# Attention scan with two gated MLPs on one core: key and query transposes on 128 rows, a new instruction order, and repeated weight checks moved to other tiles

## The chip, the cores and the metric

The kernel runs on one core of one Trainium2 chip. The metric is device time in microseconds; shown are three runs of the kernel before and one profiled execution. Engines are named as in the profile: PE (TensorE), PEld (its weight loads), DVE (VectorE), ACT (ScalarE), POOL (GpSimd), SP (SyncE, which issues most DMAs).

## The reference

Shapes: batch 4, 8 heads, 768 steps, head size 48; then 3072 tokens of width 384 through two MLPs of inner width 1536 and 2048. Inputs and weights are float32 (weights handed to the kernel as 64-bit words).

```python
mag = np.sqrt(a_re*a_re + a_im*a_im)
scale = np.minimum(mag, 0.999) / (mag + 1e-06)
a_re_n, a_im_n = a_re*scale, a_im*scale
for t in range(S):                       # S_re, S_im: [B, H, D, D]
    new_re = ar*S_re - ai*S_im           # ar, ai: row t of a_re_n, a_im_n
    new_im = ar*S_im + ai*S_re
    S_re, S_im = new_re + einsum('bhd,bhe->bhde', k[t], v[t]), new_im
    y[:, :, t] = einsum('bhd,bhde->bhe', q[t], S_re)
x = y as [tokens, 384]
xn = x / sqrt(mean(x*x) + 1e-06) * rms_g
x = (silu(xn @ w_gate) * (xn @ w_val)) @ w_out
h = x @ w_in
out = (h * clip(h + 3, 0, 6) / 6) @ w_out2
```

## The kernel before, in words

**Units.** The 768 steps are cut into seven units, each of two chunks of C steps (C is 32 in the first and last unit, 64 in the others). Inside a chunk the products of the complex factors a are accumulated forwards and backwards from its middle, so each chunk has two halves of C/2 steps. All 128 partitions work on a unit at once: a partition is one combination of half, batch, head and chunk. Before the change the partition number counts, from its highest bit down, g (batches 0-1 or 2-3), half, head parity, chunk, batch within g, and head within parity.

**Preparation of a unit (DVE and ACT).** `steps_norm` scales a; `steps_scan` runs C/2 dependent multiply-add steps (lines 442 and 446), inverts the products (`sq`, `k1`, `k2`) and forms the scaled keys and queries in two arrays P and X2 (`x1`, `x2`), of 48 real and 48 imaginary values at columns 0 to 47 and 64 to 111, hence 112 columns per step. `kwrite` writes the key part to DRAM (k_dr), and `load_k` loads it back with steps on partitions.

**Attention of a unit (`steps_G`).** `tr` turns P and X2 by TensorE: it fills one PSUM tile psT (512 columns) with eight transposes of 64 partitions (one g) by 112 columns, and ACT copies the tile to XTt (lines 597 and 603). A unit of 64-step chunks has 16 such tiles, the two short ones 8 each, 96 in all. `scores` (psS), `sums` (psU: keys times values), `state` (DVE, with a swap of the halves of the state by DMA), `outs` (psY), a normalising `scale`, and `flip` (psX: three 128-row transposes, and a split of the result into a high and a low part xh, xl) follow. psT, psS, psX and psF (the transposed chunk factors) take turns in a ring of two PSUM tiles; psU and psY share one.

**First gated projection (`steps_M`).** For each 256 tokens it multiplies by the 12 gate and value tiles, each product as three matmuls of high and low parts (`mm3`, lines 735 to 737, tile pm: 792 calls of three within the ordered part); `silu` writes the result u to DRAM.

**Order.** All of this is cut into 1680 steps, many of them generators with several parts. A string ORDER, two characters per call, gives the sequence of 2654 calls in which the parts are emitted, and the order of each engine's queue is the order of emission.

**After the units.** `steps_out1` (the first MLP's output projection) loads u in tiles uu, splits it into uh and ul (line 905), and multiplies; `steps_moe2` does the second MLP over six blocks of 512 tokens. For each of 16 inner tiles j of a block, `up` gives ph (9 matmuls), `act` computes r on ACT (line 948), r on DVE (949), gh on ACT (950) and gl on DVE (951), and `down` (9 matmuls) follows two tiles later. Tiles r, gh and gl are in rings of two. This part is ordered by the framework's scheduler.

**Checks.** The weights arrive as 64-bit words, and a check of their range (line 311: the smallest magnitude of a tile of words, to a column of wmin) guards the fast path. The gate and value weights are checked by loading them again: `recheck` loads 384 words per partition (rawc) into the ring of three buffers T1 to T3 and reduces them; 24 of these are listed beside the second MLP's blocks 1 and 2. `verdict` collects all flags and writes one column to DRAM after block 3, `verdict_end` reads it back as a row after block 4. If a flag were set, a slow fallback would run after all this.

## Time and profile before

| what | us |
|---|---|
| median of three runs | 1140.67 (1138.0 to 1144.91) |
| profiled execution | 1143.95 |
| span of its trace | 1141.9 |
| PE busy | 1061.2 (93%) |
| DVE busy | 777.4 (68%) |
| ACT busy | 543.5 (48%) |
| POOL busy | 73.9 (6%) |

The rest of the page, cut to two of its parts. The first shows busy tenths in 40 equal slices of the span, with the granted TensorE clock in tenths of full speed; the second is the chain of work that ended last, by engine.

```profile
PE   0457999999999999999999999999999999999997
...
DVE  7999999999998987868888885533333333333332
ACT  4655777758667574623334442332332333333332
...
PEclk9999999999999999999999999999999999999999
...
PE 67%; DVE 13%; issue 8%; DMA 7%; ACT 3%; POOL 1%; SPq 1%; DVEq 0%; ACTq 0%; POOLq 0%
```

A slice is 28.5 us. The first three are the preparation of the first unit, up to about the twentieth the attention of the other units runs beside the first gated projection, and then follow the output projection and the second MLP.

### The profile page before, as it was taken

Reading aid. Unit: us, or ns where it says so; the run is one execution under the profiler, and the core shown is the slowest. Engines: PE = TensorE matmul, PEld = TensorE weight load, DVE = VectorE, ACT = ScalarE, POOL = GpSimd, SP = SyncE. Lnnn points to the kernel's source line nnn. Section 1 sums busy time; section 2 is a strip of 40 time slices with the busy share of each in tenths; the row PEclk is TensorE's granted clock in tenths of the full one; section 3 lists DMA queues with packets and bytes.
Section 4 is the critical chain, followed back from the end, with each engine's and each line's share of the span. In section 5 each row is a group of like instructions: output and inputs, shape, how many; then the busy total and the mean of one; then the engine's idle time right before and its main releaser. Section 6 shows DMA issues by size and latency. Waiting matters only on the chain.

```text
span 1141.9 us, 24599 instructions
## 1 busy us (share of the span) xinstructions
PE 1061.2 (93%) x10264; PEld 926.9 (81%) x10264; DVE 777.4 (68%) x1501; ACT 543.5 (48%) x930; POOL 73.9 (6%) x99
## 2 busy tenths in 40 slices
PE   0457999999999999999999999999999999999997
PEld 0457899999998999999988886788888888888885
DVE  7999999999998987868888885533333333333332
ACT  4655777758667574623334442332332333333332
POOL 3010010000000010001222220000000000000000
PEclk9999999999999999999999999999999999999999
DMA  7525628437456365455765448601200310200000
GB/s 307 156 56 187 178 75 242 120 109 241 119 178 170 91 193 139 118 156 137 222 211 178 131 144 263 130 1 39 73 28 1 96 43 1 83 10 1 28 1 31
DMA packets 81434, 133.72 MB, mean 117 GB/s; under 512 B 32225, under 2 KB 50786, under 8 KB 80674
## 3 DMA queue, kind: packets, MB, share of 16 engines
q1 hardware_dynamic: 80658, 131.95, 39.0%
q8 instruction: 82, 1.34, 0.5%
q14 instruction: 38, 0.31, 0.1%
q10 hardware_dynamic: 656, 0.11, 0.1%
HBM read 89.77 MB, written 34.60 MB: 109 GB/s over the span
## 4 chain that ended last, share of the span: by engine, by line
PE 67%; DVE 13%; issue 8%; DMA 7%; ACT 3%; POOL 1%; SPq 1%; DVEq 0%; ACTq 0%; POOLq 0%
PE po L736 9%; PE po L737 9%; PE po L735 9%; PE pm L735 6%; PE pm L736 5%; PE pm L737 5%; PE ph L735 5%; PE ph L737 5%; PE ph L736 5%; DMA rawc<-in_wgv_dram 3%; PE psT L597 2%; PE psY L687 2%; DMA u_dr<-sg 1%; PE psS L650 1%; PE psU L667 1%
## 5 line engine op out<-in xcount | busy, mean ns | idle before, releaser
L735 PE MATMUL pm<-xh,wg 128*128 128x256 f32 x864 | 254.4, 294 | 0.5 <-ACT xh L717 0.4
L736 PE MATMUL pm<-xl,wg 128*128 128x256 f32 x864 | 245.6, 284 | 1.8 <-DVE xl L719 1.8
L737 PE MATMUL pm<-xh,wg 128*128 128x256 f32 x864 | 245.0, 284 | 0.0
L735 PEld LDWEIGHTS pm<-xh,wg 128*128 128x128 f32 x864 | 165.2, 191 | 5.8 <-issue 0.9
L736 PEld LDWEIGHTS pm<-xl,wg 128*128 128x128 f32 x864 | 165.6, 192 | 2.2 <-DVE xl L719 2.2
L737 PEld LDWEIGHTS pm<-xh,wg 128*128 128x128 f32 x864 | 165.5, 192 | 0.2
L949 DVE SCALAR_TENSOR_TENSOR r<-r,ph 128x512 f32<-128x512 f32 x96 | 65.8, 685 | 99.3 <-ACT r L948 99.1
L951 DVE TENSOR_TENSOR gl<-r,gh 128x512 fp32r<-128x512 f32 x96 | 67.5, 703 | 92.4 <-ACT gh L950 92.3
L950 ACT ACTIVATE gh<-r 128x512 fp32r<-128x512 f32 x96 | 60.7, 632 | 122.8 <-PE po L737 83.5
L948 ACT ACTIVATE r<-ph,biasz 128x512 f32<-128x512 f32 x96 | 65.8, 687 | 105.4 <-PE ph L737 105.1
L736 PE MATMUL po<-gl,w_h 128*128 128x512 f32 x288 | 113.9, 396 | 1.1 <-DVE gl L951 1.1
L737 PE MATMUL po<-gh,w_l 128*128 128x512 f32 x288 | 113.9, 395 | 0.0
L735 PE MATMUL ph<-x2b,wi_h 128*128 128x512 f32 x288 | 113.5, 395 | 0.4 <-DVE r L949 0.4
L737 PE MATMUL ph<-x2b,wi_l 128*128 128x512 f32 x288 | 113.4, 394 | 0.0
L736 PE MATMUL ph<-x2b,wi_h 128*128 128x512 f32 x288 | 113.2, 393 | 0.0
L735 PE MATMUL po<-gh,w_h 128*128 128x512 f32 x288 | 108.1, 395 | 0.0
L905 DVE TENSOR_TENSOR ul<-uu,uh 128x512 fp32r<-128x512 f32 x72 | 51.5, 717 | 73.2 <-ACT uh L904 73.1
L736 PE MATMUL po<-ul,wo 128*128 128x512 f32 x216 | 85.1, 394 | 3.0 <-DVE ul L905 3.0
L904 ACT ACTIVATE uh<-uu 128x512 fp32r<-128x512 f32 x72 | 45.4, 631 | 88.2 <-PE po L737 75.6
L737 PE MATMUL po<-uh,wo 128*128 128x512 f32 x216 | 84.7, 393 | 0.0
L442 DVE TENSOR_TENSOR m<-LAt,P 128x192 f32<-128x192 f32 x192 | 68.2, 355 | 3.9 <-ACT LAt L412 0.2
L603 ACT ACTIVATE XTt<-psT 112x512 f32<-112x512 f32 x96 | 55.2, 593 | 28.3 <-PE psT L597 27.8
(130 smaller groups left out, 1956.8 us busy)
## 6 DMA issues: line engine op xcount, KB each, us to landing
u_dr<-sg SPq DMA_DIRECT2D x72, 256.0 KB, 3.7
uu<-u_dr SPq DMA_DIRECT2D x72, 256.0 KB, 2.7
raw<-in_wo_dram SPq DMA_DIRECT2D x28, 384.0 KB, 3.6
wraw<-in_wgv_dram SPq DMA_DIRECT2D x12, 768.0 KB, 7.6
S<-in_s_all_dram SPq DMA_DIRECT2D x24, 384.0 KB, 3.8
rawc<-in_wgv_dram SPq DMA_DIRECT2D x24, 384.0 KB, 3.9
K<-k_dr SPq DMA_DIRECT2D x40, 224.0 KB, 4.2
LAt<-in_a_all_dram SPq DMA_DIRECT2D x5, 1536.0 KB, 9.4
```

What stands on the lines that cost most here:

```text
L442: tt(out=m4, in0=la, in1=pj, op=ALU.mult)
L597: nc.tensor.transpose(ps[:XW, i * 64:(i + 1) * 64], src, ident[g * 64:(g + 1) * 64, g * 64:(g + 1) * 64])
L603: nc.scalar.activation(d, s, AF.Copy)
L735: nc.tensor.matmul(ps, lhsT=wh, rhs=xh, start=first, stop=False)
L736: nc.tensor.matmul(ps, lhsT=wh, rhs=xl, start=False, stop=False)
L737: nc.tensor.matmul(ps, lhsT=wl, rhs=xh, start=False, stop=last)
L904: nc.scalar.activation(uh, uu, AF.Copy)
L905: (nc.gpsimd if n < 0 else nc.vector).tensor_tensor(out=ul, in0=uu, in1=uh.bitcast(F32), op=ALU.subtract)
L948: nc.scalar.activation(r, ph, AF.Relu, bias=biasz[:, 2:3], scale=sixth)
L949: stt(out=r, in0=r, scalar=1.0, in1=ph, op0=ALU.min, op1=ALU.mult)
L950: nc.scalar.activation(gh, r, AF.Copy)
L951: tt(out=gl, in0=r, in1=gh.bitcast(F32), op=ALU.subtract)
```

## The change

- The partition number counts half first, then g. Keys and queries of both g's for one half then lie in 64 neighbouring partitions, and `tr` transposes all 128 partitions at once: four transposes of 128 x 112 fill a psT tile. XTt has two parts (keys, queries) of 64 column groups instead of three of 32, and `col`, `kwrite` and `emit_F` index accordingly. In `steps_G` all transposes of a unit are listed before its first scores.
- ORDER is another string for another sequence of as many calls (2654).
- `recheck` loads 256 words per partition, 36 times, into the ring of tile r in the second MLP, one after each of the tiles j of blocks 1, 2 and, in part, 3. `verdict` and `verdict_end` both follow block 4.

```diff
--- before.py
+++ after.py
@@ -31,40 +31,40 @@
 
 DIGITS = "0123456789abcdefghijklmnopqrstuvwxyzABCDEFGHIJKLMNOPQRSTUVWXYZ+-"
-ORDER = (
...
+ORDER = (
...
 )
 ON_POOL = set()
 
@@ -247,7 +247,7 @@
     gcol = const.tile([128, KT], F32, name="gcol")
     flags = const.tile([128, 11 * NU], F32, name="flags")
     nc.vector.memset(flags, 0.0)
-    NW = 3 * J1 + 2 * J2
+    NW = 4 * J1 + 2 * J2
     wmin = const.tile([128, NW], F32, name="wmin")
     nc.vector.memset(wmin, 1.0)
     biasz = const.tile([128, 5], F32, name="biasz")
@@ -494,7 +494,7 @@
         def kwrite(half, sp):
             sl = slice(sp * hs, (sp + 1) * hs)
             for g in range(2):
-                p0 = g * 64 + half * 32
+                p0 = half * 64 + g * 32
                 src = P[p0:p0 + 32, 1 + sp * hs:1 + (sp + 1) * hs] if half == 0 else X2[p0:p0 + 32, sl]
                 nc.sync.dma_start(k_dr[u, g, :, half * HC + sp * hs:half * HC + (sp + 1) * hs], src)
         X = lambda f, *a: ((f.__name__,) + a, lambda: f(*a))
@@ -537,10 +537,10 @@
         return K
 
 
-    XTt = at.tile([XW, 3, 2048], F32, name="XTt")
+    XTt = at.tile([XW, 2, 4096], F32, name="XTt")
 
     def xtv(HC):
-        return XTt[:, :, 0:64 * HC].rearrange("p a (i t) -> p a i t", i=32)
+        return XTt[:, :, 0:128 * HC].rearrange("p a (i t) -> p a i t", i=64)
 
     FTp = at.tile([XW, 2, 2, 2, 8], F32, name="FTp")
     FTq = at.tile([XW, 2, 2, 2, 8], F32, name="FTq")
@@ -551,8 +551,8 @@
         nc.tensor.transpose(ps[0:IM, 128:256], Q32[:, IM:128], ident)
         nc.tensor.matmul(ps[IM:XW, 128:256], lhsT=Q32[:, 0:D], rhs=ident, start=True, stop=True)
         yield
-        FT = ps[:XW, 0:256].rearrange("p (v g a q c b h) -> p v g a q c b h", v=2, g=2, a=2, q=2, c=2, b=2)
-        fcopy = lambda out, c: [nc.scalar.activation(out[:, w], FT[:, w, :, 1, :, c].rearrange("p g q b h -> p g q (b h)"), AF.Copy) for w in range(2)]
+        FT = ps[:XW, 0:256].rearrange("p (v a g q c b h) -> p v a g q c b h", v=2, g=2, a=2, q=2, c=2, b=2)
+        fcopy = lambda out, c: [nc.scalar.activation(out[:, w], FT[:, w, 1, :, :, c].rearrange("p g q b h -> p g q (b h)"), AF.Copy) for w in range(2)]
         fcopy(FTq, 0)
         yield
         for c in range(2):
@@ -560,7 +560,7 @@
                 res.append(None)
                 continue
             F = [(FTp, FTq)[c][:, w] for w in range(2)]
-            M = [FT[:, w, :, 0, :, c].rearrange("p g q b h -> p g q (b h)") for w in range(2)]
+            M = [FT[:, w, 0, :, :, c].rearrange("p g q b h -> p g q (b h)") for w in range(2)]
             Tr = at.tile([XW, 2, 2, 2, 4], F32, name="Tr", tag=f"Tr{c}")
             Ti = at.tile([XW, 2, 2, 2, 4], F32, name="Ti", tag=f"Ti{c}")
             Tx = at.tile([XW, 4, 2, 2, 8], F32, name="Tx", tag="Tx")
@@ -589,16 +589,14 @@
             st["T"] = []
             yield from emit_F(u, st["T"])
 
-        def tr(g, w, s0):
-            SK = (2 * g - 1) * 2048
+        def tr(w, s0):
             ps = psA.tile([128, 512], F32, name="psT", tag="a")
-            for i in range(8):
-                src = P[g * 64:(g + 1) * 64, 1 + s0 + i] if w == 0 else X2[g * 64:(g + 1) * 64, s0 + i]
-                nc.tensor.transpose(ps[:XW, i * 64:(i + 1) * 64], src, ident[g * 64:(g + 1) * 64, g * 64:(g + 1) * 64])
-            d = xtv(HC)[:, 1 if w == 0 else 2 * g, 0, s0:s0 + 1]
-            d = bass.AP(d.tensor, d.offset, [list(d.ap[0]), [HC + SK if w == 0 else HC - SK, 2], [2 * HC, 32], [1, 8]])
+            for i in range(4):
+                nc.tensor.transpose(ps[:XW, i * 128:(i + 1) * 128], P[:, 1 + s0 + i] if w == 0 else X2[:, s0 + i], ident)
+            d = xtv(HC)[:, w, 0, s0:s0 + 1]
+            d = bass.AP(d.tensor, d.offset, [list(d.ap[0]), [HC + (1 - 2 * w) * 4096, 2], [2 * HC, 64], [1, 4]])
             s = ps[:XW, 0:1]
-            s = bass.AP(s.tensor, s.offset, [list(s.ap[0]), [32, 2], [1, 32], [64, 8]])
+            s = bass.AP(s.tensor, s.offset, [list(s.ap[0]), [64, 2], [1, 64], [128, 4]])
             yield
             nc.scalar.activation(d, s, AF.Copy)
 
@@ -638,8 +636,7 @@
             tt(out=so, in0=sums_(), in1=js.rearrange("p b a h e -> p b a (h e)"), op=ALU.add)
 
         def col(b, kq, hpar, c, hp):
-            return xtv(HC)[:, kq and 2 * (b // 2), hpar * 16 + c * 8 + (b % 2) * 4 + hp] if kq else \
-                xtv(HC)[:, 1, hpar * 16 + c * 8 + (b % 2) * 4 + hp]
+            return xtv(HC)[:, kq, b // 2 * 32 + hpar * 16 + c * 8 + (b % 2) * 4 + hp]
 
         def scores(b):
             psS = psA.tile([128, 512], F32, name="psS", tag="a")
@@ -718,11 +715,11 @@
             yield
             tt(out=xl[:, :, hs], in0=px, in1=xh[:, :, hs].bitcast(F32), op=ALU.subtract)
 
-        T0 = [[(("tr", g, w, s0), lambda g=g, w=w, s0=s0: tr(g, w, s0)) for w in range(2) for s0 in range(0, HC, 8)] for g in range(2)]
+        T0 = [(("tr", w, s0), lambda w=w, s0=s0: tr(w, s0)) for w in range(2) for s0 in range(0, HC, 4)]
         def kload(g, c):
             st["K", g, c] = load_k(u, g, c)
         X = lambda f, *a: ((f.__name__,) + a, lambda: f(*a))
-        front = [X(factors), X(vload), X(kload, 0, 0), X(kload, 1, 0)] + T0[0] + [X(scores, 0), X(scores, 1)] + T0[1]
+        front = [X(factors), X(vload), X(kload, 0, 0), X(kload, 1, 0)] + T0 + [X(scores, 0), X(scores, 1)]
         out = [X(swap, 0, 0), X(swap, 1, 0),
                X(sums, 0, 0), X(kload, 0, 1), X(state, 0, 0), X(swap, 0, 1),
                X(sums, 1, 0), X(kload, 1, 1), X(state, 1, 0),
@@ -844,7 +841,7 @@
 
         going = {}
         with tc.manual_schedule(engines={ET.PE, ET.DVE, ET.Activation, ET.Pool, ET.SP}):
-            seq = [i for i in range(len(steps)) for _ in range(9)] if not ORDER else [DIGITS.index(ORDER[c]) * 64 + DIGITS.index(ORDER[c + 1]) for c in range(0, len(ORDER), 2)]
+            seq = [i for i in range(len(steps)) for _ in range(11)] if not ORDER else [DIGITS.index(ORDER[c]) * 64 + DIGITS.index(ORDER[c + 1]) for c in range(0, len(ORDER), 2)]
             for i in seq:
                 now[0] = i
                 if i not in going:
@@ -930,6 +927,12 @@
 
     sixth = 1.0 / 6.0
 
+    def recheck(i):
+
+        raw = PH["mb"].tile([128, 256, 2], I32, name="rawc", tag="r")
+        nc.sync.dma_start(raw.rearrange("p n w -> p (n w)"), io["wgv"][:, i // 3].bitcast(I32).rearrange("p k n -> p (k n)")[:, i % 3 * 2 * 256:(i % 3 + 1) * 2 * 256])
+        range_check(raw, 256, i if i < 2 * J1 else NW - 3 * J1 + i)
+
     def steps_moe2(n):
         hold = {}
         out = []
@@ -972,6 +975,9 @@
                     out.append((0.65, lambda j=j, k=k: up(j, k)))
             if j < J2:
                 out.append((0.0, lambda j=j: act(j)))
+                i = J2 * (n - 1) + j
+                if 0 <= i < 3 * J1:
+                    out.append((0.0, lambda i=i: recheck(i)))
             if j >= LAG:
                 for m in range(KT):
                     out.append((0.65, lambda j=j, m=m: down(j - LAG, m)))
@@ -1019,20 +1025,13 @@
         nc.sync.dma_start(okr, ok_dr.rearrange("p n -> n p"))
         nc.vector.tensor_reduce(out=badf, in_=okr, axis=mybir.AxisListType.X, op=ALU.min)
         nc.vector.tensor_scalar(out=badi, in0=badf, scalar1=1.0, scalar2=None, op0=ALU.is_lt)
-    def recheck(i):
-
-        raw = ap.tile([128, DM, 2], I32, name="rawc", tag=f"T{(len(tiles2) + i) % 3 + 1}")
-        nc.sync.dma_start(raw.rearrange("p n w -> p (n w)"), io["wgv"][:, i // 2].bitcast(I32).rearrange("p k n -> p (k n)")[:, i % 2 * 2 * DM:(i % 2 + 1) * 2 * DM])
-        range_check(raw, DM, i)
-
     for n in range(NB):
         seq = m2[n][0] + do(m2[n][1]) if n else []
         if 1 <= n and n + 1 < NB:
             seq = do(o1[n + 1][0]) + o1[n + 1][1] + do(o1[n + 1][2]) + seq
-        run((seq, 0, 1), ([(1.0, lambda i=i: recheck(i)) for i in range(J1 * (n - 1), J1 * n)] if n in (1, 2) else [], 0, 1))
-        if n == 3:
+        run((seq, 0, 1))
+        if n == NB - 2:
             verdict()
-        if n == 4:
             verdict_end()
     eb.close()
 
@@ -1056,7 +1055,7 @@
     r = {}
     acols, scols = [], []
     p = np.arange(128)
-    g, half, hpar, c, b2, hp = p >> 6, (p >> 5) & 1, (p >> 4) & 1, (p >> 3) & 1, (p >> 2) & 1, p & 3
+    half, g, hpar, c, b2, hp = p >> 6, (p >> 5) & 1, (p >> 4) & 1, (p >> 3) & 1, (p >> 2) & 1, p & 3
     b, h = 2 * g + b2, 4 * hpar + hp
     for u, (C, t0) in enumerate(UNITS):
         HC = C // 2
```

## Rows read from the trace of the kernel before

**Rows 1.** busy us (x count) by stretch; then granted clock, DMA share, GB/s.

```profile
92.00:250.00 158.00, 153.00 (x2290) 144.07 (x2290) 153.33 (x322) 108.62 (x185) 7.45 (x14) 1.00 0.52 149
250.00:400.00 150.00, 147.75 (x2273) 140.88 (x2271) 137.91 (x294) 105.69 (x174) 6.65 (x14) 1.00 0.55 158
400.00:560.00 160.00, 157.22 (x2528) 150.39 (x2528) 126.10 (x259) 79.07 (x152) 11.98 (x22) 0.98 0.55 156
560.00:1137.00 577.00, 570.47 (x2529) 463.39 (x2527) 276.35 (x444) 201.15 (x326) 32.94 (x31) 1.00 0.26 78
```

**Rows 2.** PE's timeline around one tile psT: start us, duration us, what.

```profile
112.03 0.28 PE L737 MATMUL pm<-xh,wg 128*128 128x256 f32 x1
112.23 0.66 PE L597 MATMUL psT<-ident,X 64*112 64x64 f32 x8
...
113.05 0.28 PE L736 MATMUL pm<-xl,wg 128*128 128x256 f32 x1
```

**Rows 3.** PE's timeline around two tiles psT.

```profile
181.61 0.28 PE L736 MATMUL pm<-xl,wg 128*128 128x256 f32 x1
181.73 0.27 PE L737 MATMUL pm<-xh,wg 128*128 128x256 f32 x1
181.93 1.11 PE L597 MATMUL psT<-ident,X 64*112 64x64 f32 x16
...
183.19 0.28 PE L736 MATMUL pm<-xl,wg 128*128 128x256 f32 x1
```

**Rows 4.** PE's timeline around one psX of three 128-row transposes.

```profile
170.06 0.28 PE L737 MATMUL pm<-xh,wg 128*128 128x256 f32 x1
170.18 0.49 PE L712 MATMUL psX<-ident,Yt 128*128 128x128 f32 x3
...
170.63 0.28 PE L736 MATMUL pm<-xl,wg 128*128 128x256 f32 x1
```

**Rows 5.** PE's timeline, a GEMM instruction and the psF transpose behind it.

```profile
194.76 0.28 PE L737 MATMUL pm<-xh,wg 128*128 128x256 f32 x1
194.88 0.27 PE L550 MATMUL psF<-ident,Q 128*112 128x128 f32 x1
```

**Rows 6.** PE's timeline: GEMMs about two tiles with sums (202), about sums alone (127).

```profile
127.83 0.28 PE L737 MATMUL pm<-xh,wg 128*128 128x256 f32 x1
...
129.33 0.28 PE L736 MATMUL pm<-xl,wg 128*128 128x256 f32 x1
...
202.97 0.28 PE L737 MATMUL pm<-xh,wg 128*128 128x256 f32 x1
...
205.51 0.28 PE L736 MATMUL pm<-xl,wg 128*128 128x256 f32 x1
```

**Rows 7.** chain of waits: start us, us, what; one K write and load.

```profile
347.32 3.88 DMA k_dr<-X
351.94 5.23 DMA K<-k_dr
```

**Rows 8.** page, costliest groups: count, busy us, mean ns, idle before, releaser.

```profile
L949 DVE SCALAR_TENSOR_TENSOR r<-r,ph 128x512 f32<-128x512 f32 x96 | 65.8, 685 | 99.3 <-ACT r L948 99.1
L951 DVE TENSOR_TENSOR gl<-r,gh 128x512 fp32r<-128x512 f32 x96 | 67.5, 703 | 92.4 <-ACT gh L950 92.3
L950 ACT ACTIVATE gh<-r 128x512 fp32r<-128x512 f32 x96 | 60.7, 632 | 122.8 <-PE po L737 83.5
L948 ACT ACTIVATE r<-ph,biasz 128x512 f32<-128x512 f32 x96 | 65.8, 687 | 105.4 <-PE ph L737 105.1
```

**Rows 9.** instructions of tile rawc: count, ns min/median/max, first and last start; landings.

```profile
L311 DVE TENSOR_REDUCE wmin<-rawc x24: 546/553/555, 678.8 to 719.8; 128x1 f32<-128x384 f32 x24
...
DMA to landing us min/median/max: 3.1/3.9/5.6
```

**Rows 10.** waits of PE from 560 us: us in total, times, longest.

```profile
PE po L736 <- DVE ul L905: 3.0, 2, 1.8
PE po L736 <- DVE gl L951: 1.1, 1, 1.1
```

## What the change should do: the prediction

> **What bounds the kernel now.** I read the page's busy shares first; they are averages over three stages, so then a table of busy time by stretch [rows 1], where the busy time of TensorE (PE) and of VectorE (DVE) is to be held against each stretch's length; then single stretches of PE's timeline, the waits of PE, and the chain of waits. To about 92 us the first unit is prepared and no gated projection has started. From 92 to 560 us attention and the first gated projection run together: PE is busy 153.0 of 158, 147.8 of 150 and 157.2 of 160 us, so it idles only 5.0 + 2.3 + 2.8 = 10 us; DVE is nearly as full at first (153.3 of 158 us), then 137.9 of 150 and 126.1 of 160. From 560 to 1137 us PE has 570.5 of 577 us. So after 92 us a microsecond of PE work is worth up to a microsecond, with one reserve: up to 250 us DVE has hardly more room than PE, so that there work taken from PE alone can come back as PE's waiting for DVE.
>
> **The transposes.** A tile psT was filled by eight 64-row transposes and is now filled by four 128-row ones. There are 96 such tiles before and after; 8 belong to the first unit, before the first GEMM, and I leave them out, which leaves 88. The price of a tile is not its recorded duration (these overlap) but the delay it puts between the GEMM instructions pm around it, which otherwise start 0.12 us apart (181.61 to 181.73 [rows 3]), 0.24 for two. A lone old tile: from the pm at 112.03 to the second pm after it at 113.05 is 1.02 us, less 0.24 is 0.78 [rows 2]. Two old tiles together: 181.73 to 183.19 is 1.46, less 0.24 is 1.22 [rows 3]. The second tile costs 0.44, so the first pays 0.34 for something that is not its own work: entering and leaving 64-row operation. The new shape, 128 rows, 128 moving columns, is in the trace: three psX transposes between pm's take 170.06 to 170.63, 0.57 less 0.24 is 0.33, or 0.111 each with nothing for entering or leaving [rows 4]. Four are 0.445. The work of a tile is thus the same (0.44 before, 0.445 after: +0.4 us over 88) and only the switches go. The output has 112 columns, not 128; a 128-row 112-column transpose (psF) starts 0.12 us after the pm before it [rows 5], so it pays no switch either.
>
> How many switches? A run of instructions that are not 128-row full-width, between two pm's, is one visit. I read both order strings step by step, from the first GEMM on. With the old tiles counted as switching, the old order has 65 visits and 77 further changes of kind inside visits; with the new tiles counted as not switching, the new order has 48 visits and 39 inner changes. A visit costs 0.34. For an inner change: two tiles followed by the 64 sums matmuls delay the GEMM by 205.51 - 202.97 - 0.24 = 2.30; sums alone 129.33 - 127.83 - 0.24 = 1.26; less 0.88 for two tiles leaves 0.16 [rows 6]. Before: 65 x 0.34 + 77 x 0.16 = 34.4 us; after: 48 x 0.34 + 39 x 0.16 = 22.6. The difference is 11.8, less 0.4, so 11.4 us less PE work. The least I would defend is the lone tiles and lone pairs of the old order, 8 + 10 of them at 0.34: 6.1 us; the most, 15 us, if inner changes cost 0.25.
>
> The Trainium skill (TensorEngine Tiling (Array Packing), Performance Considerations) says that each matmul has some 60 cycles of overhead, so that a short one costs like one of 60 columns. By that, the 352 instructions that go would save another estimated 25 ns each at 2.4 GHz, 8.8 us, and the sum would be about 20 us rather than 11. The trace speaks against it: the second old tile costs 0.44 for eight, the new shape 0.445 for four [rows 2 to 4].
>
> **How much of the 11.4 us reaches the end.** Unit 1 holds 16 of the 88 tiles, before 140 us where DVE sets the pace, so 16/88 x 11.4 = 2.1 us only lets PE wait longer. Of the other 9.3 I take four fifths, 7.4: DVE has 12 us free from 250 to 400 and 34 us from 400 to 560 [rows 1] and must run that much closer to PE. Zero (DVE keeps its place) and 11.4 stay as ends.
>
> **The copies of the tiles** to SBUF (ACT, 88 of them) keep count and size; only their inner run shrinks from 8 elements to 4. I cost it at nothing: from 92 to 560 us ACT is busy 108.6 + 105.7 + 79.1 = 293 of 468 us [rows 1], and the 175 free us would hide half as much again of all its work.
>
> **The order.** All transposes of a unit now come before its first scores, and nearly all other steps are permuted. DVE's steps, each at its median row, add up to the same total in both orders, and ahead of the flips of units 2 to 5 the new order has from 7 us less to 2 us more DVE work queued. The head is alike: 314 and 313 calls before the first GEMM, so I take 0 +- 2 us there. What I can't settle by reading are the stalls: PE's 10 us of idle time could become 5 or 16. A place to watch is the round trip of the scan's k factors through DRAM: in the chain of waits a write takes 3.9 us and a load 5.2 [rows 7]. Between the last write and the first sums the new order has less PE work in units 2 and 3 (about 4 and 6 us, where the old has 7 and 8), and more in units 4 to 6. I take +0 for the order, +-5 as bounds.
>
> The writes themselves (k_dr) keep their sizes; the two of a half now start from neighbouring 32-partition strips.
>
> **The repeated checks.** Before, 24 checks of 128x384 (0.55 us each on DVE) waited in DVE's queue for their transfers, which land 3.1 to 5.6 us after issue [rows 9]; behind a waiting check stood the split of the next GEMM operand, and PE waited 3.0 us for ul and 1.1 us for gl [rows 10]: 4.1 us. After, 36 checks of 128x256 run one per tile of the second MoE. Not shown in the trace, such a check lies between 0 and 0.55 us, I take 0.41 (two thirds of the columns); 36 x 0.41 = 15 us against 24 x 0.55 = 13, with DVE idle 300 us in this stage. Spread over tiles of 18 matmuls, each check has a tile's time to land: PE's 570.5 us [rows 1] hold 2,376 of these matmuls and a few short ones, so 0.23 to 0.24 each and about 4.2 us a tile. The rectified tile r now takes every second buffer of its ring, so ACT's next r waits until gl of the tile before is done; r, r, gh, gl are about 0.69 + 0.69 + 0.63 + 0.70 = 2.7 us [rows 8], under 4.2, so it is covered; if the cover fails, each tile pays what exceeds 4.2. The last step of the verdict now follows its first directly, so DVE may wait some 8 us for a small write and read (two landings near 4 us), once, with the last block's first r and gl queued behind it; PE has two tiles of lead there, 8.4 us. I take 3.5 us of the 4.1 as gained, ends 0 and 4.1. A loss I exclude: at the longest landing of 5.6 us DVE would wait 1.4 us a tile, and it has 4.2 - 0.69 - 0.70 - 0.41 = 2.4 us free in each.
>
> **Sum.** 7.4 + 3.5 = 10.9 us off the profiled execution: its 1143.95 us (span 1141.9 and 2.05 around it) become 1133. It was 3.3 us over the median of 1140.67, so the median should be 1129.8: 1130.
>
> **Rivals.**
> - *DVE keeps the pace* (0.21): PE's saved time turns into waits for DVE in 92 to 560 us, since the new order keeps DVE's work and its sequence of units. For it: DVE at 97% to 250 us. Against: 46 us of DVE idle from 250 to 560 [rows 1]. Then only the checks pay: 1140.67 - 3.5 = 1137 (1134 to 1141).
> - *K's round trip binds, slower* (0.11): the sums of each unit stand in PE's queue before GEMMs that are ready; if the two writes of a half from adjacent strips take twice their 3.9 us, each of six units loses up to 3.9, 23 us in all: 1130 + 23 = 1153. It decides once write and load exceed the PE work between them, which at 9 us they nearly do in units 2 and 3. Against it: transfers of the same size.
> - *The new transposes still switch* (0.06): 112 of 128 columns count as another shape. The new order scatters its tiles, 117 visits and 46 inner changes with them: 117 x 0.34 + 46 x 0.16 = 47.1 against 34.4, +12.7, less 3.5: 1150. Against it: psF [rows 5].
> - *Price by instruction* (0.04): if a tile's cost goes with its count, four 64-row prices of 0.055 each are 0.22 instead of 0.445, up to 88 x 0.22 = 19 us more gain; half of that is 1120. The skill's overhead rule above points there.
> - The forecast: 0.58, its own range 1124 to 1136.
>
> **The numbers.** Three runs span 1138.0 to 1144.9, so 0.5% (5.7 us) is about what can be told from no change: faster is below 1135, slower above 1146.4. Faster: 0.55 of the forecast, 0.06 of the DVE rival, 0.04 of the price rival: 0.66 with a rest. Same: 0.21, most from the DVE rival. Slower: 0.13 from the two slow ones. The range that leaves out 2 in 10 takes in the forecast, the DVE rival and the price rival: 1119 to 1143.
>
> **What would show it.** A lone new tile should delay the GEMM by 0.44 to 0.45 us, not 0.78; if it is near 0.8, the switch argument fails. From 92 to the end of attention PE's busy time should shrink by about 11 us with its idle time near 10; busy down but idle up by as much means DVE, and sums waiting for K mean the round trip. After 560 us no wait of PE for ul should stand, and the checks should spread over more than 100 us instead of 41. If the stretch to the first GEMM moves by over 3 us, the order did something that I have not priced.

## The result and the profile after

The changed kernel took 1154.42 us (median of 6 runs, 1151.17 to 1157.98) where the kernel before, run beside it, took 1140.55: a ratio of 1.0115, 95% interval 1.0096 to 1.0135, about 13 us slower. Forecast was 1130, and 1119 to 1143 as the range. The profiled execution took 1157.98 us, its span 1156.1. Every kernel below was timed beside runs of the kernel before; kernels are compared by their ratio to those runs, in us as (ratio − 1) x 1141, with the 95% interval in brackets. A profile is one execution and only says where.

The busy time by stretch, of the kernel after; columns as in [rows 1], the last stretch 14 us longer as the kernel is.

```profile
92.00:250.00 158.00, 146.12 (x2173) 137.28 (x2171) 152.44 (x323) 108.12 (x185) 9.85 (x16) 0.99 0.53 145
250.00:400.00 150.00, 143.06 (x2161) 137.16 (x2160) 135.79 (x287) 108.31 (x177) 9.61 (x14) 0.99 0.56 153
400.00:560.00 160.00, 148.00 (x2293) 140.96 (x2293) 116.67 (x239) 74.25 (x141) 10.80 (x20) 0.97 0.49 136
560.00:1151.00 591.00, 582.83 (x2693) 475.76 (x2691) 297.56 (x492) 209.36 (x340) 34.87 (x32) 1.00 0.28 82
```

From 92 to 560 us PE idles 11.9 + 6.9 + 12.0 = 30.8 us; it was 10 [rows 1]. The first GEMM starts later: its first instruction, PE's timeline, was at 93.21 and is here at 99.28, but PE has other work up to there, and only 3.8 of the 30.8 us lie before it.

```profile
99.28 0.58 PE L732 MATMUL pm<-xh,wg 128*128 128x256 f32 x1 [0.42 <-ACT xh L714]
```

What PE waited for in the changed kernel, 92 to 600 us (total, times, longest). The silu and product of the gated projection (sg) stand first, in no wait of the kernel before.

```profile
PE pm L732 <- ACT sg L752: 8.5, 7, 3.1
PE psX L709 <- ACT Yt L700: 5.5, 3, 2.8
PE psU L664 <- DMA K<-k_dr: 4.1, 4, 2.1
PE psY L675 <- ACT Yt L700: 2.5, 2, 1.9
PE pm L732 <- DVE sg L754: 2.3, 5, 1.1
```

A single tile costs what the prediction says. One lone and two together, PE's timeline after, to be read as [rows 2] and [rows 3]:

```profile
108.70 0.28 PE L734 MATMUL pm<-xh,wg 128*128 128x256 f32 x1
108.82 0.60 PE L595 MATMUL psT<-ident,X 128*112 128x128 f32 x4
109.18 0.37 PE L732 MATMUL pm<-xh,wg 128*128 128x256 f32 x1
109.38 0.28 PE L733 MATMUL pm<-xl,wg 128*128 128x256 f32 x1
...
110.65 0.28 PE L734 MATMUL pm<-xh,wg 128*128 128x256 f32 x1
110.77 0.60 PE L595 MATMUL psT<-ident,P 128*112 128x128 f32 x4
111.20 0.60 PE L595 MATMUL psT<-ident,X 128*112 128x128 f32 x4
...
111.76 0.28 PE L733 MATMUL pm<-xl,wg 128*128 128x256 f32 x1
```

Lone: 109.38 − 108.70 − 0.24 = 0.44 us (0.78 before); two: 111.76 − 110.65 − 0.24 = 0.87 (1.22 before). PE's work is shorter, and the time longer.

The checks (instructions of rawc, then PE's waits from 575 us) answer to [rows 9] and [rows 10]: 0.42 us each instead of 0.55, over 194 us instead of 41, and PE's wait for ul shrinks from 3.0 to 0.2; the one for gl (1.1) is gone. A wait of 2.8 us for uh, which the kernel before has not, takes part of this back.

```profile
L311 DVE TENSOR_REDUCE wmin<-rawc x36: 409/420/422, 733.1 to 927.3; 128x1 f32<-128x256 f32 x36
DMA to landing us min/median/max: 2.6/2.7/4.7
```

```profile
PE po L732 <- ACT uh L901: 2.8, 1, 2.8
PE po L733 <- DVE ul L902: 0.2, 1, 0.2
```

### The profile page after: what moved, and what is told of

It reads as the page before. It is cut to its first block, busy times and chain, and to the rows that moved or that the text cites. A ratio compares the mean times of both kernels' runs of the same rounds, so it can differ in the third digit from the quotient of the medians.

```text
span 1156.1 us, 23851 instructions
## 1 busy us (share of the span) xinstructions
PE 1049.1 (91%) x9880; PEld 915.5 (79%) x9880; DVE 781.9 (68%) x1513; ACT 544.9 (47%) x930; POOL 85.1 (7%) x99
## 5 line engine op out<-in xcount | busy, mean ns | idle before, releaser
L733 PE MATMUL pm<-xl,wg 128*128 128x256 f32 x864 | 242.3, 280 | 0.0
L734 PE MATMUL po<-uh,wo 128*128 128x512 f32 x216 | 84.7, 393 | 0.0
L732 PE MATMUL po<-uh,wo 128*128 128x512 f32 x216 | 66.3, 394 | 2.8 <-ACT uh L901 2.8
```

Source lines behind the costliest of these rows:

```text
L732: nc.tensor.matmul(ps, lhsT=wh, rhs=xh, start=first, stop=False)
L733: nc.tensor.matmul(ps, lhsT=wh, rhs=xl, start=False, stop=False)
L734: nc.tensor.matmul(ps, lhsT=wl, rhs=xh, start=False, stop=last)
```

## The experiments

**Each part alone.** The first four kernels ran side by side (the kernel before: 1143.05).

*c_only*: the kernel before with the moved checks.

```
+ steps_moe2: out.append((0.0, lambda i=i: recheck(i)))   # 36 of 128x256
- 24 checks of 128x384 between the second MLP's blocks
```

> The kernel before with only the repeated checks moved as in the change (36 of 256 words in the ring of r, verdict after block 4). Prediction's term: 3.5 us less, 1137 us; PE's waits for ul and gl after 560 us gone. Rival: the scheduler's order of the second MLP shifts and the time stays within 1 us of 1140.5.

1140.83 us, 0.9977 [0.9957, 0.9998]: −2.6 us.

*t_old*: the new order and checks with the 64-row tiles. Each new tile's place takes an old tile; keys of the first two batches are overwritten too early in it, so part of the result is another.

```
  ORDER of after, ("tr", w, s0) -> ("tr", g = 0 if s0 % 8 == 0 else 1, w, s0 // 8 * 8)
```

> The kernel before with the new order and the new checks but the old 64-row transposes and the old partition order (each new tile's place emits one old tile). By the price of switches PE has 23 us more work than in the changed kernel. Theory 1 in its plain form (PE's time adds up): 1170 to 1178 us. If the new order leaves PE waiting for other engines in the same places, part of it hides: 1158 to 1168 us. Rival (the transposes make the waits): at or below 1148 us.

1162.9 us, 1.0170 [1.0136, 1.0203]: +19.4 us. The order alone, 1.0170 − 0.9977, costs 22.0 us with the old tiles; the new tiles then give 1.0170 − 1.0115, 6.3 us back.

*o_old*: the new tiles in an order that I derived from the old one, the pairs of new tiles at the places of the first half's old ones.

```
  old order; ("tr", 0, w, s0) -> ("tr", w, s0), ("tr", w, s0 + 4) at once; ("tr", 1, ...) dropped
```

> The changed kernel with the old order put back: each old 64-row tile of the first batch half now emits a pair of 128-row tiles at its place, the old places of the second half are left out, all other calls stand as before the change; transposes, layout and checks are the changed ones. Theory 1 (the new order costs, the transposes pay): the 11 us of waits gained by PE in the changed trace go, the saved PE work of 10 us stays: 1128 to 1138 us, first GEMM near 93 us. Rival (the transposes themselves make the waits, as all of a unit's must stand before its first scores): 1145 to 1155 us, idle PE time in the attention stage near 30 us instead of 9.

1175.91 us, 1.0286 [1.0249, 1.0322]: a miss. PE waited 20.1 us (26 times) at psT for the copies of tiles (XTt): the psT ring holds two tiles, and mine came in pairs. It says nothing of the tiles, but much of orders made by hand.

**The head.** POOL's normalising factor of the first unit took 0.78 us at 69.41 in the kernel before (L697); POOL's timeline after, and DVE's end of the same stretch:

```profile
71.45 6.70 POOL L694 TENSOR_SCALAR ms<-flags 64x1 f32<-64x1 f32 x1 [61.43 <-ACT Yt L692]
78.24 1.92 POOL L695 TENSOR_TENSOR ms<-ms,cst 64x1 f32<-64x1 f32 x1
```

```profile
73.62 0.94 DVE L403 SCALAR_TENSOR_TENSOR T<-T,T 128x768 f32<-128x768 f32 x1
74.48 0.34 DVE L442 TENSOR_TENSOR m<-LAt,P 128x192 f32<-128x192 f32 x1
74.75 1.00 DVE L406 SCALAR_TENSOR_TENSOR LAt<-LAt,cst,T 128x768 f32<-128x768 f32 x1
75.68 0.24 DVE L446 TENSOR_TENSOR P<-m 128x96 f32<-128x96 f32 x1
75.85 0.94 DVE L631 TENSOR_TENSOR JS<-JS,Ti 112x768 f32<-112x768 f32 x1
76.72 0.34 DVE L442 TENSOR_TENSOR m<-LAt,P 128x192 f32<-128x192 f32 x1
76.99 0.94 DVE L303 SCALAR_TENSOR_TENSOR wdA<-wraw,wdA 128x768 int32<-128x768 int32 x1
77.86 0.24 DVE L446 TENSOR_TENSOR P<-m 128x96 f32<-128x96 f32 x1
78.03 0.41 DVE L651 TENSOR_TENSOR At<-psS,mask 64x256 f32<-64x256 f32 x1
```

A 64x1 operation lasts 6.7 us and ends when DVE, after a run of instructions without a gap, nearly all with two operands in SBUF, starts one (At) that takes an operand from PSUM. *warm* tested whether it is POOL's first use.

```
+ nc.gpsimd.tensor_scalar(out=warm..., ...); nc.gpsimd.tensor_tensor(out=warm..., op=ALU.pow)   # early, on a tile of its own
```

> The changed kernel with two small POOL instructions (multiply-add and power on 64x1, result unused) behind POOL's first memsets. In the changed trace POOL's first multiply-add took 6.7 us (0.78 before the change) at 71 us, on the way to the first GEMM, which starts 6.0 us later than before. If that is what a first use of the operation costs POOL in this program: first GEMM near 93 us and 1147 to 1150 us. Rival (the head is late for another reason of the order, and POOL's long span only fills a wait): 1152 to 1156 us, first GEMM still near 99 us.

1154.93 us, 1.0104 [1.0072, 1.0137], and the operation took 6.71 us at 71.62: first use falls. *ms0* moves the first unit's factors to ACT:

```
+ if u == 0: nc.scalar.activation(ms0, fy, AF.Ln, scale=1/DM, bias=1e-6); nc.scalar.activation(ms1, ms0, AF.Exp, scale=-0.5)
```

> The changed kernel with the first unit's four normalising factors (multiply-add and power on POOL) computed on ACT by logarithm and exponential. Theory on the head: POOL's small instruction took 6.7 us at 71 us because DVE ran two-input SBUF instructions without a break until 78 us; off POOL, the first GEMM starts 5 to 7 us earlier, near 93 us, and the time falls to 1146 to 1150 us. Rival (the head waits for DVE's own work, POOL's wait only fills it): first GEMM within 2 us of 99 us, 1152 to 1156 us.

1148.7 us, 1.0051 [1.0033, 1.0069]: 5.7 us below the kernel after by medians, 7.3 by ratios. The first GEMM, PE's timeline of ms0, comes back to nearly its old place:

```profile
94.79 0.58 PE L737 MATMUL pm<-xh,wg 128*128 128x256 f32 x1 [0.42 <-ACT xh L719]
```

So the operation stood on the way to the first GEMM. The Trainium skill (SBUF — State Buffer, Who interferes with whom) says that a DVE instruction with two SBUF inputs contends with a GpSimd instruction that reads SBUF, and that the loser is blocked fully, for the whole instruction. The trace agrees in part: the operation lasted over fourteen DVE instructions, and not over one. What held it so long is not shown. In the kernel before it also started beside a DVE instruction with two SBUF operands, and was through after 0.78 us although DVE went on with more of them without a gap (POOL's timeline before, then DVE's):

```profile
69.41 0.78 POOL L697 TENSOR_SCALAR ms<-flags 64x1 f32<-64x1 f32 x1 [59.39 <-ACT Yt L695]
...
69.03 0.95 DVE L633 TENSOR_TENSOR JS<-JS,Ti 112x768 f32<-112x768 f32 x1
69.89 0.25 DVE L446 TENSOR_TENSOR P<-m 128x96 f32<-128x96 f32 x1
70.06 0.48 DVE L328 SCALAR_TENSOR_TENSOR wg<-wdA,gcol,wg 128x256 fp32r<-128x256 f32 x1
```

**What the new tiles ask of the order.** A new tile holds rows of all batches for 4 positions, so no scores can start before all 16 tiles of a unit are out; before, 8 were enough. *late* is the old order with the 64-row tiles and only that added: 110 calls wait, and what depends on them. *late_T* is the same sequence of calls with the new tiles. (In late the same keys are overwritten early as in t_old.)

```
  late:   old order; ("scores", b) and its dependents held until all ("tr", ...) of the unit are done
  late_T: the same calls, ("tr", g, w, s0) -> ("tr", w, s0 + 4 * g)
```

> The kernel before with the moved checks (1138 us by c_only) and its own order, in which the scores of a unit and what depends on them (110 calls) wait until all 16 tiles of the unit are out, as the new transposes demand; transposes are the old ones. (The keys of the first two batches are overwritten before they are read, so this part of the result is another one.) Theory 1 (a bad order is the whole cost, the demand itself is free): 1136 to 1141 us. Theory 2 (scores that must wait for all tiles cost by themselves): 1146 to 1156 us, PE's idle time in the attention stage up by 8 us or more.

> The same order as the kernel late, call by call, with the new transposes, partition order and layout in the places of the old ones: the clean pair for the transposes alone. By the price of switches (65 visits and 77 inner changes against some 50 and 40) 9 to 12 us less PE work than late: theory 1: 1126 to 1131 us, faster than before. Theory 2: 4 to 12 us under late, 1138 to 1148 us. If the transposes gave nothing (rival: what they save comes back as waits): within 2 us of late.

late: 1199.62 us, 1.0506 [1.0447, 1.0566], +58 us; late_T: 1192.43, 1.0437 [1.0399, 1.0474]. That demand, met by mere waiting, costs far more than the tiles can give. Only about half of it is waiting: for the other half PE is busy longer with the same instructions, at a lower granted clock (0.92 of full speed over the stage, 1.00 in c_only; rows further down). The tiles are worth 7.9 us in this pair, though the two intervals overlap and the clock differs here too (0.96 in late_T).

*free_T* takes the demand away: the new tiles at the old places, scores as early as before.

```
  old order; ("tr", g, w, s0) -> ("tr", w, s0 + 4 * g); XTt cleared once on POOL
```

> The changed kernel's tiles and checks, with the order of the kernel before call by call: each 128-row tile stands where a 64-row tile stood, and the first scores of a unit start after 8 of its 16 tiles, as before. They so read columns that the other 8 tiles have not written yet, so part of the result is another; the buffer is cleared once at the start. Theory A (what costs time is that the new tiles let no score start before all 16 are out, and the order that follows from it; the tiles themselves gain): the switches go and nothing else moves, so the kernel before with only the checks moved (1140.8 us) less 7 to 11 us, 1130 to 1134. Rival B (PE's saved time is waited away whatever the order, because DVE keeps the pace): 1138 to 1143. Rival C (the new tiles or their copies hold something up by themselves): over 1146. The profile should show by A: PE busy in the attention stage about 10 us below the kernel before, idle within 5 us of its 9.4, POOL's first normalising factor at 0.8 us and not 6.7.

1138.96 us, 0.9982 [0.9967, 0.9997]: no different from c_only. Theory A missed. A flaw was mine: late tiles overwrote columns that the unit's first outputs still read, and 8 copies stood 13.9 us behind psY in ACT's queue. *free_2* gives the late tiles a buffer of their own.

```
+ if s0 % 8: d = XTd[...]   # copy of a late tile; scores read zeros there
```

> The new tiles in the old order, as in the earlier run of that order, but the 8 tiles of each unit that come after its first scores are copied to a buffer of their own instead of to columns that those scores and outputs have read. In the earlier run 8 of these copies stood 13.9 us in ACT's queue behind psY, which no copy does in the kernel before; that wait came from my placing them so, not from the tiles. The scores then read zeros for these columns (part of the result is another) and no longer wait for these copies, which may flatter it by up to the 1.8 us that scores waited for copies before. Theory A (the copies behind psY had taken the saving back; the tiles themselves gain once nothing new waits): 1130 to 1134, a ratio of 0.990 to 0.994. Rival B (the shorter trips take it, whatever the copies do): the ratio of the earlier run, 0.998, within 0.002: 1137 to 1141.

1138.82 us, 0.9966 [0.9950, 0.9983], 1.3 us below c_only, inside either interval: the flaw was not it. Two of PE's largest waits, 92 to 600 us, c_only first, then free_2:

```profile
PE pm L736 <- DVE xl L719: 2.0, 2, 1.5
...
PE psU L667 <- DMA K<-k_dr: 1.4, 3, 0.8
```

```profile
PE psU L668 <- DMA K<-k_dr: 6.3, 7, 1.7
```

From its first GEMM to its last PE is busy 4.3 us less (463.3 to 459.0, rows further down) and idles 7.2 more; 4.9 of that is K. The tiles stood in PE's queue between the write of the k factors and the sums that wait for their load. My reading was that the work that went had been the cover of this wait; the next pairs test it.

**What takes the saving back.** Two suspects, each made lighter in c_only and in free_T, so that each pair differs by the tiles alone: K's write (from the third unit on the load takes the second unit's place in DRAM, so the k factors are another unit's), and DVE's load (the recurrence's product over half its columns, another recurrence). Names with c_ have the old tiles, with free_ the new ones; k, lite and lk are the first edit, the second and both.

```
k:    - kd = k_dr[u, g, ...]            + kd = k_dr[min(u, 1), g, ...]
lite: - tt(out=m4, in0=la, in1=pj)      + tt(out=m4[:, :, 0], in0=la[:, :, 0], in1=pj[:, :, 0])
      - tt(out=pn, m4[.., 0] + m4[.., 1]) + tt(out=pn, in0=m4[:, :, 0], in1=pj[:, :, 0], op=max)
```

> The kernel before with the moved checks, and from the third unit on the k factors are loaded from the second unit's place in DRAM, so that no load waits until the unit's own write has landed; those units thus use another unit's k factors, and part of the result is another. It is the partner of the next kernel. TensorE waited 1.4 us for K in this kernel without that edit (1140.8 us), so both theories expect 1138 to 1141.

> The same edit on the kernel with the new tiles in the old order (1139.0 us, in which TensorE's work was 11 us shorter and its idle time 14 us longer, 5.5 of it for K). Theory A (the saved PE work is taken back by the round trip of the k factors, which has less PE work to lie beside): 4 to 7 us below its partner, 1132 to 1136. Rival B (DVE and ACT keep the pace, K is only where it shows): within 2.5 us of its partner, 1137 to 1142, with the waits for K gone and others, for XTt, Sst, At and P, grown.

> The kernel before with the moved checks, and DVE's work in the attention stage made lighter: the product of each step of the recurrence (m, 128x192, 355 ns) is taken over half its columns, so that it should take what the 128x96 sum beside it takes, 254 ns; some 190 of them, 155 from 92 to 560 us, about 16 us less of DVE's work there. The recurrence is thus another, and with it the result. It is the partner of the next. TensorE idles 17 us in that stretch without the edit (1140.8 us): 1130 to 1139 by either theory.

> The same edit on the kernel with the new tiles in the old order. Theory A (DVE keeps the pace, so the PE work saved by the new tiles can't come through): with DVE lighter it does, 4 to 10 us below its partner. Rival B (what takes the saving back lies beside PE and ACT: the two-buffer ring of the tiles, the copies, the clock): within 2.5 us of its partner.

> Both edits on the kernel before with the moved checks: the lighter recurrence and, from the third unit on, the k factors from the second unit's place. Its partner without the second edit took 1129.3 us with 1.1 us of waits for K: 1125 to 1130.

> Both edits on the kernel with the new tiles in the old order. With the lighter recurrence alone it took 1131.5 us, 2 over its partner, and its profile had 11 us more of PE's waits: 5.0 more for K, 3.2 more for the tiles' copies. Theory A (the PE work that went was the cover of the K load and of a few shorter trips, and K's is the largest part): with the write's landing out of K's trip it is 2 to 5 us below its partner. Rival B (the shorter trips take it whatever K does): within 1.5 us of its partner or over it, with XTt, At and Sst waits grown again.

| edit | old tiles | new tiles | new − old, us |
|---|---|---|---|
| none | 0.9977 (c_only) | 0.9982 (free_T), 0.9966 (free_2) | +0.6, −1.3 |
| k | 0.9949 [0.9933, 0.9966], 1138.17 us | 0.9936 [0.9921, 0.9952], 1136.62 | −1.5 |
| lite | 0.9886 [0.9857, 0.9915], 1129.32 | 0.9904 [0.9878, 0.9930], 1131.53 | +2.1 |
| both | 0.9866 [0.9840, 0.9893], 1128.3 | 0.9891 [0.9866, 0.9915], 1129.44 | +2.9 |

Rival B three times over: with K's write out of the way, with DVE lighter, with both, the new tiles gain nothing in this order; every difference lies inside the intervals. The k edit did not take the load itself away: PE's waits for K fell from 5.5 us (free_T) to 3.3 (free_k) and from 6.1 (free_lite) to 3.3 (free_lk), and were 2.1 and 2.6 in the old-tile partners c_k and c_lk. So K's write is refuted as the whole cause, K's load is not tested. The pairs carry free_T's flaw, so they don't show what free_2 would do with K's wait gone; that pair was not run. A lighter DVE is itself worth 10 us to the old tiles: DVE's product went from 355 to 257 ns, some 15 us less DVE work in that stretch. In the profiled executions 4.6 us of the gain lie before the first GEMM (at 95.51 in c_only, 90.88 in c_lite), so not all of it bears on the stage where the tiles are.

**The rest of the new order's cost**, each on ms0: a third sg buffer, K's write, the lighter DVE.

```
ms0_sg3:  + sg = mo.tile(..., tag="sg", bufs=3)     (Tx shares the tile of m4)
ms0_k, ms0_lite: the edits above
```

> The changed kernel with the first unit's normalising factors on ACT (1148.7 us), and three buffers instead of two for the gated product sg (a scratch tile of the factors moves into another tile's buffer to make room). Theory A (the new order costs in the attention stage because GEMM, silu and product meet in two buffers of sg and of pm: TensorE waited 8.5 us for ACT's silu and 2.3 for DVE's product): 4 to 10 us off, 1139 to 1145. Rival B (these waits only show that ACT and DVE are late, since ACT's queue stands 42 us behind psY): within 3 us of 1148.7, the waits of pm on sg still over 6 us.

> The changed kernel with the first unit's normalising factors on ACT (1148.7 us), and from the third unit on the k factors from the second unit's place in DRAM, as above (part of the result is another). Theory A (K's round trip binds in the new order): the 4.1 us of TensorE's waits for K go, 1143 to 1146. Rival B: another wait takes their place, 1146.5 to 1150.

> The same edit on the changed kernel with the first unit's normalising factors on ACT (1148.7 us). Theory A (the new order is slower because DVE's work is queued at the wrong places, and its share of idle time says little): 8 to 16 us off, 1133 to 1141, with TensorE's waits for sg and Yt falling by half. Rival B (ACT's queue standing behind psY, which DVE does not set): 0 to 5 us off, 1144 to 1149.

ms0_sg3: 1146.9 us, 1.0021 [1.0003, 1.0040], 3.4 below ms0 by ratios, 1.8 by medians; between the theories. PE's waits of pm for sg, 10.7 us in ms0, stayed at 6.3 and moved from ACT to DVE (the profiled execution is its fastest, 1141.48):

```profile
PE pm L737 <- DVE sg L759: 6.0, 6, 3.2
...
PE pm L737 <- ACT sg L757: 0.3, 1, 0.3
```

ms0_k: 1149.53, 1.0040 [1.0020, 1.0060], 1.3 below: rival B; PE's waits for K fell only from 3.8 to 2.7 us. ms0_lite: 1138.84, 0.9967 [0.9949, 0.9985], 9.6 below, the number of theory A. But the old order gained 10.4 by the same edit, and the waits for sg did not halve (9.0 against 10.7), though those for Yt did (3.7 against 8.4): the gain is DVE's in either order, and the gap between the orders stays, 0.9967 − 0.9886 = 9 us.

**PE's stage as a whole.** A fixed window favours a kernel that runs late, since its work moves out at the window's end. So here is each kernel from the start of its first GEMM to that of its last; columns as in [rows 1]. In order: before, c_only, t_old, after, free_2, c_lite, free_lite, late, late_T.

```profile
93.20:577.80 484.60, 475.20 (x7232) 452.74 (x7233) 432.79 (x897) 298.21 (x517) 32.73 (x56) 0.99 0.55 157
95.51:573.34 477.83, 463.33 (x7231) 440.16 (x7232) 429.94 (x893) 296.21 (x515) 30.71 (x54) 1.00 0.56 157
101.22:600.51 499.29, 482.00 (x7232) 449.56 (x7232) 430.43 (x892) 298.15 (x516) 36.02 (x55) 0.99 0.53 149
99.30:594.70 495.40, 464.71 (x6880) 442.40 (x6880) 429.03 (x888) 296.94 (x515) 35.35 (x54) 0.98 0.54 149
96.89:577.51 480.62, 458.95 (x6879) 437.14 (x6880) 431.92 (x895) 296.39 (x515) 32.89 (x55) 0.99 0.56 156
90.88:566.99 476.11, 465.28 (x7231) 443.12 (x7232) 417.72 (x897) 297.18 (x516) 32.69 (x55) 0.99 0.57 159
91.72:570.33 478.61, 457.35 (x6880) 434.52 (x6881) 417.42 (x896) 296.58 (x515) 32.60 (x55) 0.99 0.57 157
95.69:637.64 541.95, 496.84 (x7231) 469.68 (x7232) 433.41 (x895) 297.96 (x515) 29.38 (x55) 0.92 0.49 139
95.68:627.81 532.13, 473.32 (x6879) 449.10 (x6880) 432.72 (x895) 297.56 (x515) 30.18 (x55) 0.96 0.51 141
```

PE idles for the difference of the first two columns behind the window: 9.4, 14.5, 17.3, 30.7, 21.7, 10.8, 21.3, 45.1 and 58.8 us.

- The kernel before and c_only have the same stage, yet PE is busy 475.2 and 463.3 us. In the profiled execution of the kernel before the GEMM's three lines last 281, 280 and 280 ns (medians), in the eight others 276. Why is open. So c_only is the base for PE's work, not that profile.
- The order with the old tiles (c_only to t_old): PE is busy 18.7 us more, idles 2.8 more, and starts 5.7 later. That is mostly work, not waiting: by the prediction's own prices, with its 117 visits and 46 inner changes, the new order has 47.1 − 34.4 = 12.7 us more switches as long as the tiles are of 64 rows; the granted clock is 0.99 and not 1.00.
- The new tiles in the new order (t_old to after): 17.3 us less work, 13.4 more idle. In the old order (c_lite to free_lite, at the same mean clock): 7.9 less work, 10.4 more idle. In either order most or all of what the tiles save comes back as waits.
- late against c_only: the same 7231 instructions keep PE busy 33.5 us longer, at a granted clock of 0.92, and PE idles 30.6 us more.

c_only, the old transposes and order with the moved checks, is the one kernel here that computes the whole reference and beats both, the kernel before by 2.6 us.

## Why the prediction was wrong

The sum in ratios, by kernels that differ in one part: checks −2.6; order on the old tiles +22.0; tiles in the new order −6.3; together +13.1. The other way round: checks −2.6, tiles in the old order −1.3 (free_2, whose result is another), order on the new tiles +17.0 (1.0115 − 0.9966). Either chain ends at the total by its making; that its terms differ shows that tiles and order are not additive.

- **The order: the step that failed**, "I take +0 for the order, +-5 as bounds". It cost 17 to 22 us, and this alone turns the sign. Where the prediction let PE's 10 us of idle time become 5 or 16, PE idles 30.7 us in the stage (14.5 in c_only), and it starts 4 to 6 us later. I had summed DVE's and PE's work ahead of the same marks and found differences of a few us; what I did not follow is when the scores may start. The scores' instructions, kernel after (ns min/median/max, first and last start):

```profile
L647 PE MATMUL psS<-XTt x896: 196/222/270, 62.6 to 543.3; 112*64 112x64 f32 x128, 112*32 112x32 f32 x52
```

They began at 46.7 in the kernel before and begin at 62.6. From the last step that makes a unit's queries to its first scores the kernel before takes 6 to 18 us in units 1 to 6 and this one 15 to 35; in units 1 to 5 what follows, scores to the first flip, is pressed from 18 to 24 us into 8 to 15. ACT then stands in its queue before the squares of psY (ACT's waits, 92 to 560 us; 15.2 us before), and the silu behind it comes late:

```profile
ACT Yt L692 <- PE psY L684: 43.3, 20, 13.0
```

  Shown is that the order costs this much, with either tiles, and that the new tiles' demand on the scores costs time where nothing else is done about it (late, +58, about half of it PE's longer work at the lower clock). That this demand is what makes PE idle in the new order is argued only: in t_old, where the scores start as late and ACT waits 39.0 us before the squares of psY, PE idles only 17.3 us, with 17.3 us more work to do. Nor is the chain through Yt and sg shown to be the whole of the 9 to 10 us left in the attention stage: a third buffer gave back 2 to 3.
- **The head, "0 +- 2 us"**: 6.1 us later than in the profile before, 3.8 later than in c_only's, 5.7 to 7.3 in the time. I counted calls and did not look at POOL's instruction on the way.
- **The transposes' price**: right to 0.02 us for a tile (0.44 lone, 0.87 for two, 0.445 and 0.89 forecast). Over the stage the forecast was 11.4 us less PE work. The two profiles seem to bear it out (475.2 to 464.7, 10.5), but this is luck: the profile before ran each GEMM instruction slower, and against c_only PE's busy time did not shrink (463.3). What the tiles alone took off is 7.9 us in the old order and 17.3 in the new one.
- **How much reaches the end, 7.4**: that the new order shows 6.3 is luck as well. The forecast let two thirds of 11.4 us through; there it was 6.3 of 17.3, and in late 7.9 of 23.5, with a difference in the clock in it. In the old order that I reasoned from it was −1.3 to +0.6: the saving came back as waits, in free_2 4.9 us of them K's.
- **The copies**: 597 ns before and after, and ACT had room; nothing for it, as forecast.
- **The checks**: 3.5 forecast, 2.6 measured; PE's new wait for uh (2.8 us, 2.2 in c_only) was not foreseen. A check was forecast at 0.41 us and measured at 0.42, by a slip: two thirds of 0.55 is 0.37, and a third fewer columns saved only a quarter of the time.
- **DVE keeps the pace** (0.21, 1137) describes the old order well in its time (free_2 1138.8); its cause is not borne out: a lighter DVE is worth 10 us, but doesn't let the tiles' saving through. **K's round trip** (0.11, 1153) had the right sign, and its 1153 lies near the 1154.42, but not by its mechanism: the writes' landings did not double (medians of 3.7 us before, 3.7 and 4.1 after), PE waited 4.1 us for K in all, and loading from an older write in ms0_k gave 1.3 us. **Still switch** and **price by instruction** are refuted by the rows of the tiles above.
- **What would show it**: "busy down but idle up by as much means DVE" was too quick; the idle time was waits for sg, Yt and K. "If the stretch to the first GEMM moves by over 3 us, the order did something that I have not priced" held: it moved 6.

What stays open: whether another order pays for the new tiles' demand, which waits make the 9 us in the attention stage, and how much of the 13 us is the granted clock (0.98 over the stage in after, 1.00 in c_only), which no run here held fixed.

## What to carry to other kernels

An order of instructions can't be priced at zero because its queues hold equal amounts of work: look at what a changed tile asks for (here all 16 tiles before the first scores), and how long each unit's chain waits for it. Work taken from an engine that is 97% busy can come back as waits: 7.9 us less in the old order gave nothing, 17.3 less in the new one gave 6. Read a stage from its own first to its own last instruction, and check that two profiles run a common instruction equally fast before taking one's busy time from the other's. Price an edit in two orders before trusting either, and run the cheap part of a change by itself: here it was the only part that paid.

## What the runs showed of the hardware

A 64x1 POOL operation that reads SBUF took 0.78 us in one order and 6.70 us in another; in both, DVE ran instructions with two SBUF operands back to back beside it, and what held it is open. Four transposes of 128 rows cost PE 0.44 us and eight of 64 rows also 0.44, plus 0.34 us for each visit to the smaller shape. A DVE product over 96 instead of 192 columns took 257 instead of 355 ns: half the columns saved 28%. In late, the same PE instructions as in c_only took 496.8 instead of 463.3 us of PE's time at a mean granted clock of 0.92 instead of 1.00.
